# A windowed-attention and SwiGLU kernel: the opening's first loads, its attention with V stationary for six chunks, and its order rewritten

## The chip, the cores and the metric

The kernel runs on one NeuronCore of one Trainium2 chip. The metric is the device time of one execution in microseconds (us); lower is better. Engines are named as in the profile: PE (TensorE, matrix products), PEld (its weight loads), DVE (VectorE), ACT (ScalarE), POOL (GpSimd, which here makes the mask and issues the loads from HBM) and SP (SyncE, which issues the stores and the DMA transposes).

## The reference

Sliding-window causal attention over 8 sequences of 576 positions, 8 heads of 64, followed by a gated feed-forward block over the 4608 tokens. All inputs and the output are fp32.

```
scores = (q @ k^T) / 8, masked to 0 <= i - j < 64, softmax over j
x   = (softmax @ v), heads side by side: 4608 x 512
out = (silu(x @ w_gate) * (x @ w_val)) @ w_out        d_ff = 1536
```

## The kernel before

**Tiles.** The 4608 tokens are 36 chunks of 128 and nine token blocks of 512 (four chunks each). Matrix operands are bf16; the loads on POOL's queue convert on the way in.

**The steps of a chunk n**, each a method, with the lines that the profile shows:
- `load_qk`, `load_v` (L320, L382): three loads from HBM on POOL's queue. Chunks 0 and 1 differ: `first_loads` (L326) brings k and q of both as two fp32 transfers on SP's and ACT's queues, `first_cast` (L339, L337) converts them on DVE and ACT, `first_T` (L349) transposes them on PE.
- `T` (L407) transposes k and q on PE, with a copy out of PSUM on DVE or ACT (L339, L337); from chunk 8 on, `TD` (L420, L423) does it by two DMA transposes on SP's queue.
- `bias` (L431) writes the mask's large negative numbers into two PSUM banks ahead of the scores; it is used for chunks 0 to 3. Otherwise the mask is a multiplication on DVE after the exponential (L466).
- `S` (L451): 24 score matmuls on 64x64 quarters of the array into two banks; two exponentials on ACT (L461) give `pt`, keys on partitions.
- `A` (L500): 32 matmuls with `pt` stationary and V (with a column of ones) moving, so that queries lie on partitions and column 64 is the denominator. `A(n, n + 1)` puts the scores of the next chunk between its two halves. On DVE a reciprocal of four columns and a multiplication per half (L515, L518) give `xb`.
- `X` (L532) transposes `xb` on PE, with a copy to `xT` on ACT (L541); `XD` (L547) does it by a DMA transpose.

**The feed-forward part.** `F(c, f, t0, t1)` does one of twelve 128-wide slices of d_ff for tokens t0 to t1 of block c: four matmuls for gate and four for value (L565), then a tanh on ACT (L571) and two operations on DVE (L573, L575), which give `hT`. `O(c, u)` multiplies 128 tokens of `hT` by w_out in 12 matmuls (L589), copies on ACT (L601) and stores on SP's queue (L603). PSUM has eight banks; `banks` sets which are used in turn by attention ("a") and by F ("f").

**The order** is written out by hand in `build`, as a list of calls. Each engine runs its instructions in this order; a small planner in the kernel adds the semaphore waits that the tiles need. For blocks 0 and 1 the calls stand one by one; from block 2 on a loop places one chunk of attention, four chunks ahead, between F and O. `W(a, b)` loads gate and value slices a to b, `load_wo` loads w_out. Matmuls on zeros (`warm`, L368) run before the first data.

Of the kernel before, what the change touches and what calls it, by code (L numbers as in the profile page):

```python
# [5 lines left out]
ALU = mybir.AluOpType  # L6
# [188 lines left out]
class _Kernel:  # L195
# [8 lines left out]
    NO = 4  # L204

# [7 lines left out]
    def alloc(self):  # L213
# [20 lines left out]
        self.fq, self.fk = [sb(x, H * 128, F32)[:, :].rearrange("p (h j d) -> p h j d", h=H, j=2) for x in ("fq", "fk")]  # L234
        self.cq, self.ck = [sb(x, H * 128)[:, :].rearrange("p (j h d) -> p j h d", j=2, h=H) for x in ("cq", "ck")]
# [66 lines left out]
    def init_mask(self):  # L302
        for p0, c0, op in ((0, 0, ALU.is_ge), (0, 64, ALU.is_gt), (64, 0, ALU.is_gt), (64, 64, ALU.is_ge)):
            d = self.nmask[p0:p0 + 64, c0:c0 + 64]
            sg = 1 if op == ALU.is_gt else -1
            self.g.op("pool", lambda e, d=d, op=op, sg=sg: e.affine_select(
                out=d, in_=d, compare_op=op, fill=-30000.0, base=0,
                pattern=[[-sg, 64]], channel_multiplier=sg), writes=["nmask"])
        self.g.op("dve", lambda e: e.tensor_scalar(self.mask[:, :], self.nmask[:, :], -1.0, None, ALU.is_ge),
                  reads=["nmask"], writes=["mask"])  # L310
# [11 lines left out]
    def first_loads(self):  # L322
        for eng, dst, src, nm in (("sp", self.fk, self.k, "fk"), ("act", self.fq, self.q, "fq")):
            d = dst.rearrange("p h j d -> p h (j d)")
            a = src[0, :, 0:256, :].rearrange("h (p j) d -> p h (j d)", j=2)
            self.g.op(eng, lambda e, d=d, a=a: e.dma_start(d, a), writes=[nm], dma=True)  # L326

    def first_cast(self, which, half, eng):
        dst, src = (self.ck, self.fk) if which == "k" else (self.cq, self.fq)
        hs = slice(0, 8) if half is None else slice(4 * half, 4 * half + 4)  # L330
        d = dst[:, :, hs].rearrange("p j h d -> p h j d")
        wk = [("c" + which, i) for i in range(2) if half in (None, i)]
        self.move(eng, d, src[:, hs], ["f" + which], wk)
# [7 lines left out]
    def first_T(self, which):  # L341
        bank, bk = self.bank("a")
        tb = bank[:, :].bitcast(BF).rearrange("p (c j t) -> p c j t", c=4, j=2)
        src = self.ck if which == "k" else self.cq

        def pe(e):
            for pr in range(4):
                for j in range(2):
                    r = e.transpose(tb[:, pr, j, :], src[:, j, 2 * pr:2 * pr + 2, :], self.ident[:, :])  # L349
            return r  # L350

        self.g.op("pe", pe, reads=["ident", ("c" + which, 0), ("c" + which, 1)], writes=[bk])
# [42 lines left out]
    def T(self, n, keng="act"):  # L395
# [3 lines left out]
        parts = [("kn", self.kn[iq], kd, kk, keng), ("qn", self.qn[iq], self.qT[iz], qk, "act")]  # L399
        for group in ([parts] if keng == "act" else [parts[:1], parts[1:]]):  # L400
# [34 lines left out]
    def S(self, n, bb=None, defer=False):  # L435
# [33 lines left out]
        for f in masks:  # L469
            f()  # L470

# [78 lines left out]
    def F(self, c, f, t0=0, t1=512):  # L550
        g = self.g
        it, ih = c % self.NX, c % self.NH
        xT, hT = self.xT[it], self.hT[ih]
        i = self.n_s % self.NS
        self.n_s += 1
        sig, uu = self.sig[i], self.uu[i]
        n = t1 - t0
        xk = [("xT", it, u) for u in range(t0 // 128, t1 // 128)]
        G, gk = self.bank("f")
        V, vk = self.bank("f")  # L560
# [9 lines left out]
        g.op("pe", mm(G, self.Wg), reads=xk + [("Wg", f)], writes=[gk])  # L570
        g.op("act", lambda e: e.activation(sig[:, 0:n], G[:, 0:n], ACTF.Tanh, scale=0.5), reads=[gk], writes=[("sig", i)])  # L571
        g.op("pe", mm(V, self.Wv), reads=xk + [("Wv", f)], writes=[vk])
# [180 lines left out]
    def build(self):  # L753
# [7 lines left out]
        self.first_loads()  # L761
# [15 lines left out]
        self.load_v(4)
        load(5)
        W(10, 12)
        load(6)  # L780
        load(7)

        self.banks("a", [5, 6, 7, 4, 0, 1])
        self.warm(13)
        self.first_cast("k", None, "dve")
        self.first_cast("q", 0, "act")
        self.first_cast("q", 1, "dve")
        tk = self.first_T("k")
# [163 lines left out]
```

## Time and profile before

| | us |
|---|---|
| runs shown | 338.45, 336.24, 336.99 (median 336.99) |
| the profiled execution, its own time | 338.46 |
| its span, first to last instruction | 336.6 |
| first real matmul (transposes of chunk 0 and 1) | 6.94 |
| first F (0,0) | 14.01 |
| A(4,5) | 37.37 |
| F(2,0), first of the third token block | 86.99 |

How to read it: a timeline row gives start, duration, engine, line, operation, output and inputs, shape and count, and in brackets the idle time before it with what ended that. A row of the groups gives busy time in us and the mean in ns of one, then the idle time before. A row of windows gives for each engine the busy time and, after the five engines, the granted TensorE clock (1.00 is full), the busy share of the DMA engines and GB/s. A PE row's duration includes its drain, so back-to-back rows overlap.

### The profile page before, as it was taken

The numbers are of one execution on the slowest core, as the hardware profiler recorded it, in microseconds if no ns is written. First come the engines' busy times: TensorE is split into PE (matmuls) and PEld (weight loads), VectorE is DVE, ScalarE is ACT, GpSimd is POOL, SyncE is SP. The second block draws the span as 40 slices with busy tenths as digits, with TensorE's granted clock in tenths as the row PEclk, the third lists the DMA queues.
The fourth block names the chain that finished last, engine by engine and source line by source line (L and its number), as shares of the span: only waits on it lengthen the run. The fifth ranks groups of instructions, "written<-read, shape, count | busy, mean of one in ns | idle before, by whom it ended". The sixth has DMA issues, their size and how long they took to land.

```text
span 336.6 us, 8417 instructions
## 1 busy us (share of the span) xinstructions
PE 325.6 (97%) x3515; PEld 166.1 (49%) x3515; DVE 215.6 (64%) x481; ACT 140.1 (42%) x256; POOL 111.1 (33%) x141
## 2 busy tenths in 40 slices
PE   6979999998999999999999999999999999999995
PEld 3548567644444444444444444444444444444444
DVE  5548789478667766666666666666666665566510
ACT  2645874354444544443433344433443332332311
POOL 7999993463544353333343333000000000000000
PEclk9979999999999999999999999999999999999999
DMA  9999999999999999999999999334331111000012
GB/s 170 143 186 171 167 195 160 154 177 128 172 179 180 177 154 166 162 168 127 125 80 149 139 139 126 80 79 80 78 80 49 47 49 49 31 32 34 34 65 95
DMA packets 169516, 40.20 MB, mean 119 GB/s; under 512 B 155904, under 2 KB 164992, under 8 KB 169472
## 3 DMA queue, kind: packets, MB, share of 16 engines
q0 software_dynamic: 117312, 18.36, 77.6%
q1 hardware_dynamic: 50976, 20.66, 34.0%
q10 hardware_dynamic: 1184, 0.59, 0.7%
q8 instruction: 29, 0.48, 0.5%
q14 instruction: 15, 0.12, 0.2%
HBM read 37.75 MB, written 9.44 MB: 140 GB/s over the span
## 4 chain that ended last, share of the span: by engine, by line
PE 87%; DMA 4%; POOL 4%; DVE 2%; ACT 1%; issue 1%; SPq 0%; POOLq 0%
PE ps L565 53%; PE ps L589 26%; PE ps L500 4%; DMA qT<-qn 2%; PE ps L451 2%; DMA Wv<-in_moe_w_val_dram 2%; POOL va L382 1%; PE ps L617 1%; POOL Wg L388 1%; PE ps L407 1%; POOL Wv L388 1%; POOL qn L320 1%; POOL kn L320 1%; DVE uu L573 0%; PE ps L532 0%
## 5 line engine op out<-in xcount | busy, mean ns | idle before, releaser
L573 DVE SCALAR_TENSOR_TENSOR uu<-sig,ps 128x512 bf16<-128x512 bf16 (+2 forms) x122 | 76.1, 624 | 82.6 <-ACT sig L571 82.4
L565 PE MATMUL ps<-xT,Wg 128*128 128x512 bf16 (+2 forms) x488 | 114.1, 356 | 2.0 <-DMA Wg<-in_moe_w_gate_dram 0.9
L565 PE MATMUL ps<-xT,Wv 128*128 128x512 bf16 (+2 forms) x488 | 113.8, 356 | 0.7 <-DMA Wv<-in_moe_w_val_dram 0.7
L589 PE MATMUL ps<-Wo,hT 128*128 128x512 bf16 x420 | 95.9, 379 | 0.0
L571 ACT ACTIVATE sig<-ps 128x512 bf16<-128x512 f32 (+2 forms) x122 | 66.9, 549 | 61.6 <-PE ps L565 61.1
L575 DVE SCALAR_TENSOR_TENSOR hT<-uu,ps 128x512 bf16<-128x512 bf16 (+2 forms) x122 | 76.3, 625 | 5.2 <-PE ps L565 1.0
L565 PEld LDWEIGHTS ps<-xT,Wv 128*128 128x128 bf16 x488 | 47.3, 98 | 47.7 <-DMA Wv<-in_moe_w_val_dram 1.0
L589 PEld LDWEIGHTS ps<-Wo,hT 128*128 128x128 bf16 x420 | 41.0, 98 | 48.9
L565 PEld LDWEIGHTS ps<-xT,Wg 128*128 128x128 bf16 x488 | 43.9, 98 | 42.3 <-DMA Wg<-in_moe_w_gate_dram 1.0
L320 POOL DMA_DIRECT2D qn<-in_q_dram x38 | 35.1, 941 | 85.9 <-DMA qT<-qn 85.6
L601 ACT ACTIVATE ost<-ps 128x512 f32<-128x512 f32 x35 | 20.9, 597 | 95.1 <-PE ps L589 92.2
L461 ACT ACTIVATE pt<-ps 128x512 bf16<-128x512 f32 x72 | 38.9, 595 | 22.6 <-PE ps L451 22.6
L382 POOL DMA_DIRECT2D va<-in_v_dram x40 | 37.2, 940 | 1.0 <-issue 0.6
L320 POOL DMA_DIRECT2D kn<-in_k_dram x38 | 35.0, 927 | 5.0 <-DMA Wo<-in_moe_w_out_dram 4.0
L518 DVE TENSOR_TENSOR xb<-ps,rc 128x256 bf16<-128x256 f32 x72 | 30.6, 425 | 2.5
L466 DVE TENSOR_TENSOR pt<-pt,mask 128x512 bf16<-128x512 bf16 x64 | 24.1, 417 | 0.2 <-ACT pt L461 0.2
L500 PE MATMUL ps<-va,pt 64*64 64x65 bf16 x1088 | 23.3, 199 | 0.6
L500 PEld LDWEIGHTS ps<-va,pt 64*64 64x64 bf16 x1088 | 15.3, 109 | 16.1 <-issue 11.2
L515 DVE RECIPROCAL rc<-ps 128x4 f32<-128x4 f32 x72 | 12.6, 175 | 9.9 <-PE ps L500 9.9
L451 PE MATMUL ps<-qT,kT 64*64 64x64 bf16 (+1 forms) x864 | 15.9, 201 | 1.0 <-DMA qT<-qn 1.0
L451 PEld LDWEIGHTS ps<-qT,kT 64*64 64x64 bf16 x864 | 12.6, 108 | 3.1 <-DMA qT<-qn 1.2
L339 DVE COPY ost<-ps 128x128 f32<-128x128 f32 x1 | 0.3, 291 | 11.8 <-PE ps L617 11.8
(50 smaller groups left out, 72.5 us busy)
## 6 DMA issues: line engine op xcount, KB each, us to landing
out_dram<-ost SPq DMA_DIRECT2D x35, 256.0 KB, 3.1
va<-in_v_dram POOLq DMA_DIRECT2D x32, 128.0 KB, 9.9
qn<-in_q_dram POOLq DMA_DIRECT2D x30, 128.0 KB, 11.2
kn<-in_k_dram POOLq DMA_DIRECT2D x30, 128.0 KB, 10.0
Wo<-in_moe_w_out_dram POOLq DMA_DIRECT2D x2, 768.0 KB, 17.4
Wg<-in_moe_w_gate_dram POOLq DMA_DIRECT2D x5, 256.0 KB, 8.0
Wv<-in_moe_w_val_dram POOLq DMA_DIRECT2D x5, 256.0 KB, 9.1
fk<-in_k_dram SPq DMA_DIRECT2D x1, 512.0 KB, 5.4
```

What stands on the lines that cost most here:

```text
L320: self.g.op("pool", lambda e, d=d, a=a: e.dma_start(d, a), writes=ks, dma=True)
L382: g.op("pool", lambda e, d=d, a=a: e.dma_start(d, a), writes=ks, dma=True)
L451: r = e.matmul(sv[h][o:o + 64, c, q0:q1], self.kT[ps, c, kk:kk + 64], qT[ps, c, q0:q1], start=not biased, stop=not biased or c == 3 and kk ...
L461: g.op("act", lambda e, po=po, si=si: e.activation(po, si, ACTF.Exp, scale=SCALE), reads=[bk], writes=[pk])
L466: "dve", lambda e: e.tensor_tensor(po, po, m, ALU.mult), reads=[pk, "mask"], writes=[pk]))
L500: r = e.matmul(av[half][ws, j, :], pt[ks, h, ws], vv[ks, h, 0:65], start=key == q[0], stop=key == q[-1])
L518: g.op("dve", lambda e, xo=xo, rb=rb, a=av[half]: e.tensor_tensor(xo, a[:, :, 0:64], rb, ALU.mult), reads=[bk, ("rc", ir)], writes=[("xb", ...
L565: r = e.matmul(bank[:, 0:n], W[:, kk, f * 128:f * 128 + 128], xT[:, kk, t0:t1], start=(kk == 0), stop=(kk == NK - 1))
L571: g.op("act", lambda e: e.activation(sig[:, 0:n], G[:, 0:n], ACTF.Tanh, scale=0.5), reads=[gk], writes=[("sig", i)])
L573: g.op("dve", lambda e: e.scalar_tensor_tensor(uu[:, 0:n], sig[:, 0:n], 1.0, G[:, 0:n], ALU.add, ALU.mult), reads=[("sig", i), gk], writes ...
L575: g.op("dve", lambda e: e.scalar_tensor_tensor(hT[:, f, t0:t1], uu[:, 0:n], 0.5, V[:, 0:n], ALU.mult, ALU.mult), reads=[("uu", i), vk], wr ...
L589: r = e.matmul(OB[:, :], hT[:, f, 128 * u:128 * u + 128], self.Wo[:, f, :], start=(f == 0), stop=(f == NF - 1))
```

## The change

- **First loads.** Four transfers in place of two: k and q of chunk 0, then of chunk 1. One fp32 tile `fx` holds k on partitions 0 to 63 and q on 64 to 127 for one chunk. `open_T` transposes it by ordinary matmuls against half of the identity, into two fp32 banks; `open_ev` copies them to `kT` and `qT`.
- **The mask** is one select on POOL and two operations on DVE in place of four selects.
- **V stationary.** For chunks 0, 1, 2, 3, 6 and 7, `open_A` replaces `A` and `X`: V is the stationary operand and `pt` moves, so the result already lies as `xT` needs it. The denominators come from matmuls with ones, broadcast over 64 partitions: a 128x512 bank, whose reciprocal DVE takes whole (`dn`); two multiplications write `xT`. 32 matmuls of one column and a reciprocal of eight columns fill `rc`, which only a later check of the denominators reads.
- **Chunks 6 and 7** get their mask by `bias`, and their scores no longer stand inside another chunk's `A`. **Chunks 8 and 9** are transposed by PE (`T`) and no longer by `TD`.
- **F.** With at most 256 tokens, gate and value share one bank. With `defer`, the matmuls are issued where F stands and the work on ACT and DVE where `Fev` stands.
- **The order** of blocks 0 and 1, with the order of the loads, is written anew. Values and weights come in another order: two more weight transfers, chunk 8 behind w_out.

The diff, cut to its core; the removed calls of `build` are those printed above:

```diff
-        self.fq, self.fk = [sb(x, H * 128, F32)[:, :].rearrange("p (h j d) -> p h j d", h=H, j=2) for x in ("fq", "fk")]
-        self.cq, self.ck = [sb(x, H * 128)[:, :].rearrange("p (j h d) -> p j h d", j=2, h=H) for x in ("cq", "ck")]
+        self.fx = [t[:, :].rearrange("p (h j d) -> p h j d", h=H, j=2) for t in ring("fx", self.NG, H * 128, F32)]
+        self.cx = [t[:, :].rearrange("p (j h d) -> p j h d", j=2, h=H) for t in ring("cx", self.NG, H * 128)]
+        self.dn = ring("dn", 2, 512, F32)
...
+        g, nm = self.g, self.nmask
+        big = -2.0 ** 30
+        g.op("pool", lambda e: e.affine_select(
+            out=nm[:, :], in_=nm[:, :], compare_op=ALU.is_ge, fill=big, base=0,
+            pattern=[[1, 128]], channel_multiplier=-1), writes=["nmask"])
+        for p0 in (0, 64):
+            a = nm[p0:p0 + 64, p0:p0 + 64]
+            d = nm[p0:p0 + 64, 64 - p0:128 - p0]
+            g.op("dve", lambda e, d=d, a=a: e.tensor_scalar(d, a, -1.0, big, ALU.mult, ALU.add), reads=["nmask"], writes=["nmask"])
+        g.op("dve", lambda e: e.tensor_scalar(self.mask[:, :], nm[:, :], -1.0, None, ALU.is_ge),
+             reads=["nmask"], writes=["mask"])
...
+    def open_load(self, n, eng, which):
+        src, p0 = (self.k, 0) if which == "k" else (self.q, 64)
+        i = n % self.NG
+        d = self.fx[i][p0:p0 + 64].rearrange("p h j d -> p h (j d)")
+        a = src[0, :, 128 * n:128 * n + 128, :].rearrange("h (p j) d -> p h (j d)", j=2)
+        self.g.op(eng, lambda e: e.dma_start(d, a), writes=[("fx", i, which)], dma=True)
+
+    def open_cast(self, n, h0, h1, eng):
+        i = n % self.NG
+        d = self.cx[i][:, :, h0:h1].rearrange("p j h d -> p h j d")
+        self.move(eng, d, self.fx[i][:, h0:h1], [("fx", i, "k"), ("fx", i, "q")], [("cx", i, h) for h in range(h0, h1)])
...
+    def open_T(self, n):
+        i = n % self.NG
+        src = self.cx[i]
+        got = []
+        for w in range(2):
+            bank, bk = self.bank("a")
+            tb = bank[:, :].rearrange("p (c j t) -> p c j t", c=4, j=2)
+
+            def pe(e, tb=tb, w=w):
+                for pr in range(4):
+                    for j in range(2):
+                        r = e.matmul(tb[:, pr, j, :], src[:, j, 2 * pr:2 * pr + 2, :], self.ident[:, 64 * w:64 * w + 64],
+                                     start=True, stop=True)
+                return r
+
+            self.g.op("pe", pe, reads=["ident"] + [("cx", i, h) for h in range(H)], writes=[bk])
+            got.append((tb, bk))
+        return got
+
+    def open_ev(self, n, got, keng="dve", qeng="act"):
+        for (tb, bk), d, nm, eng in ((got[0], self.kT[:, :, 64 + 128 * n:192 + 128 * n], "kT", keng), (got[1], self.qT[n], "qT", qeng)):
+            a = tb.rearrange("p c j t -> p c t j")
+            self.move(eng, d.rearrange("p c (t j) -> p c t j", j=2), a, [bk], [(nm, n, p) for p in range(4)])
...
+    def open_A(self, n):
+        g = self.g
+        ip, it, u = n % self.NP, n // 4, n % 4
+        va, vp, pt = self.va[n % self.NV], self.va[(n - 1) % self.NV], self.pt[ip]
+        db, dk = self.bank("a")
+        bb = [self.bank("a") for _ in range(2)]
+        den = db[:, :].rearrange("p (c q) -> p c q", c=4)
+        out = [b[:, 0:256].rearrange("p (j q) -> p j q", j=2) for b, _ in bb]
+        tot = bb[0][0][:, 256:264]
+        po = pt.rearrange("p (c e) q -> p c e q", e=2)
+        lo = 0 if (2 * n) % BPB else 64
+        hi = 128 if (2 * n + 1) % BPB else 64
+        count, done = {}, {}
+
...
+        def den_seq(kp):
+            ks, qq = span(kp)
+            qq = qq if part else [slice(0, 128)]
+            return [(("d", e), den[64 * e:64 * e + 64, 2 * i:2 * i + 2, q], self.ones[ks, 0:64], po[ks, 2 * i:2 * i + 2, e, q])
+                    for i in range(2) for q in qq for e in range(2)]
+
+        def out_seq(step):
+            seq = []
+            for j in range(2):
+                for half in range(2):
+                    kp = half ^ step
+                    ks, qq = span(kp)
+                    c = 2 * half + j
+                    cuts = [(q, vp if kp and q.start == 0 else va) for q in qq]
+                    for e in range(2):
+                        for q, vv in cuts:
+                            seq.append(((half, e), out[half][64 * e:64 * e + 64, j, q], vv[ks, 2 * c + e, 0:64], po[ks, c, e, q]))
+            return seq
+
+        def tot_seq(kp):
+            ks = span(kp)[0]
+            return [((0, w), tot[64 * w:64 * w + 64, h:h + 1], pt[ks, h, 64 * w:64 * w + 64], self.ones[ks, 0:1])
+                    for h in range(H) for w in range(2) if kp == w or (2 * n + w) % BPB]
+
+        parts = [(den_seq(0), [dk]), (out_seq(0) + tot_seq(0), None), (den_seq(1), [dk]), (out_seq(1) + tot_seq(1), None)]
...
+        near = (n - 1, n) if n else (n,)
+        vk = [("va", m % self.NV, j) for m in near for j in range(2)] + [("va", m % self.NV) for m in near]
+        pk = [("pt", ip, 0), ("pt", ip, 1), "ones"]
+        ok = [bk for _, bk in bb]
+        prev = None
+        order = []
+        for i, (seq, wk) in enumerate(parts):
+            order.append(g.op("pe", run(seq), reads=pk + ([] if wk else vk), writes=wk or ok,
+                              after=[order[i - 2]] if i >= 2 else []))
+        dn = self.dn[n % 2]
+        g.op("dve", lambda e: e.reciprocal(dn[:, :], db[:, :]), reads=[dk], writes=[("dn", n % 2)])
+        dv = dn[:, :].rearrange("p (c q) -> p c q", c=4)
+        for half, (_, bk) in enumerate(bb):
+            cs = slice(2 * half, 2 * half + 2)
+            xo = self.xT[it][:, cs, 128 * u:128 * u + 128]
+            g.op("dve", lambda e, xo=xo, half=half, cs=cs: e.tensor_tensor(xo, out[half], dv[:, cs, :], ALU.mult),
+                 reads=[bk, ("dn", n % 2)], writes=[("xT", it, u)])
+        rc = self.rc[:, 8 * n:8 * n + 8]
+        g.op("dve", lambda e: e.reciprocal(rc, tot), reads=[ok[0]], writes=[("rc", 2 * n), ("rc", 2 * n + 1)])
...
+        if n <= 256:
+            G, gk = self.bank("f")
+            V = G[:, 256:512]
+            vk = gk
+        else:
+            G, gk = self.bank("f")
+            V, vk = self.bank("f")
...
+        g.op("pe", mm(V, self.Wv), reads=xk + [("Wv", f)], writes=[vk])
+        if defer:
+            return (c, f, t0, t1, i, G, gk, V, vk)
+        self.F_ev(c, f, t0, t1, i, G, gk, V, vk)
+
+    def F_ev(self, c, f, t0, t1, i, G, gk, V, vk):
...
-        self.first_loads()
+        self.open_load(0, "sp", "k")
+        self.open_load(0, "act", "q")
+        self.open_load(1, "sp", "k")
+        self.open_load(1, "sp", "q")
         self.init()
         self.init_pool_a()
         self.init_mask()
         self.load_v(0)
+        W(0, 1)
         self.load_v(1)
+        load(2)
         W(1, 2)
+        load(3)
+        W(2, 3)
+        W(3, 4)
+        W(4, 6)
+        load(4)
+        W(6, 8)
+        load(5)
         W(8, 10)
         W(10, 12)
         load(6)
         load(7)
         self.load_wo(0, 6)
         self.load_wo(6, 12)
+
+        def pre(n, *cast):
+            for h0, h1, eng in cast or ((0, 8, "dve"),):
+                self.open_cast(n, h0, h1, eng)
+
+        def att(n):
+            if n in self.FAST:
+                self.open_A(n)
+            else:
+                self.A(n)
+                self.X(n, "act")
+
+        def F(f, t0, t1, c=0):
+            held.append(self.F(c, f, 128 * t0, 128 * t1, True))
+
+        def Fev():
+            for h in held:
+                self.F_ev(*h)
+            held.clear()
+
+        held = []
+        bs = {}
+        self.banks("a", [5, 6, 7, 4, 0, 1])
+        self.banks("f", [2, 3])
+        self.warm(13)
+        pre(0, (0, 5, "dve"), (5, 8, "act"))
+        t = self.open_T(0)
+        bs[0] = self.bias(0)
+        self.open_ev(0, t)
+        self.S(0, bs[0])
+        self.warm(2)
+        pre(1)
+        t = self.open_T(1)
+        self.open_ev(1, t)
+        att(0)
+        bs[1] = self.bias(1)
+        self.S(1, bs[1])
+        F(0, 0, 1)
+        self.T(2, "dve", "act")
+        att(1)
+        Fev()
+        bs[2] = self.bias(2)
+        self.S(2, bs[2])
+        F(0, 1, 2)
+        F(1, 0, 2)
+        self.T(3, "dve", "act")
+        att(2)
+        Fev()
+        bs[3] = self.bias(3)
+        self.S(3, bs[3])
+        self.banks("f", [0, 1, 2, 3])
+        self.banks("a", [5, 6, 7, 4])
+        F(0, 2, 3)
+        F(1, 2, 3)
+        att(3)
+        Fev()
+        self.F(0, 2, 0, 384)
+        self.F(0, 3, 0, 384)
+        self.F(0, 0, 384, 512)
+        self.F(0, 1, 384, 512)
+        self.F(0, 2, 384, 512)
+        self.F(0, 3, 384, 512)
+        load(8)
         load(9)
+        self.F(0, 4)
         self.T(4)
         load(10)
+        self.F(0, 5)
+        self.S(4)
         self.F(0, 6)
+        self.F(0, 7)
         self.T(5)
         load(11)
+        self.F(0, 8)
         self.A(4, 5)
+        self.F(0, 9)
+        self.F(0, 10)
+        self.X(4, "act")
+        self.T(6, "dve", "act")
         load(12)
+        self.A(5)
+        self.F(0, 11)
+        self.T(7, "act", "dve")
         self.X(5, "act")
+        self.banks("a", [4, 5, 0, 1, 6, 7])
+        self.banks("f", [2, 3])
+        bs[6] = self.bias(6)
+        self.S(6, bs[6])
+        bs[7] = self.bias(7)
+        F(0, 0, 2, 1)
+        Fev()
+        self.S(7, bs[7])
+        F(1, 0, 2, 1)
+        att(6)
+        Fev()
+        F(2, 0, 2, 1)
+        att(7)
+        Fev()
+        self.banks("a", [4, 5, 0, 1])
+        self.banks("f", [3, 6, 7, 2])
+        F(3, 0, 2, 1)
+        for f in range(4):
+            F(f, 2, 4, 1)
+            Fev()
+        load(13)
+        self.T(8)
+        self.F(1, 4)
         self.S(8)
         self.TD(10)
         self.TD(11)
+        self.T(9)
+        self.F(1, 5)
+        self.O(0, 0, None, "f")
+        load(14)
+        self.A(8, 9)
+        self.XD(8)
+        self.TD(12)
+        self.F(1, 6)
+        self.O(0, 1, None, "f")
+        load(15)
+        self.A(9, 10)
+        self.XD(9)
+        self.TD(13)
+        self.F(1, 7)
+        self.F(1, 8)
+        load(16)
+        self.A(10, 11)
+        self.TD(14)
+        self.O(0, 2, None, "f")
+        self.X(10, "act")
+        self.F(1, 9)
+        load(17)
+        self.A(11, 12)
+        self.TD(15)
+        self.F(1, 10)
+        self.O(0, 3, None, "f")
+        self.X(11, "act")
+        self.F(1, 11)
...
```

177 lines of the change are left out of this document (38 added, 139 removed).

## The prediction

> **What bounds the kernel now.** I read the page's busy times and clock row first, then its chain of work that ended last, then a window that holds the opening's slow stretch and one that holds the rest.
>
> ```profile
> PE 325.6 (97%) x3515; PEld 166.1 (49%) x3515; DVE 215.6 (64%) x481; ACT 140.1 (42%) x256; POOL 111.1 (33%) x141
> ...
> PEclk9979999999999999999999999999999999999999
> ...
> PE 87%; DMA 4%; POOL 4%; DVE 2%; ACT 1%; issue 1%; SPq 0%; POOLq 0%
> ```
>
> ```profile
> 20.00:25.00 5.00, 4.13 (x80) 2.68 (x79) 2.59 (x10) 0.71 (x3) 5.00 (x8) 0.66 1.46 196
> 80.00:330.00 250.00, 249.92 (x2399) 118.09 (x2400) 159.36 (x325) 96.90 (x167) 50.34 (x60) 1.00 0.95 105
> ```
>
> From 80 us on TensorE is busy 249.92 of 250.00 us at full clock, and the change leaves that part as it is. Whatever happens must happen before the first pass of the third token block, F(2,0). So I compare when that pass starts, and carry the difference to the end. The first 80 us have these waits in the timeline of TensorE (bracketed), and these landmarks:
>
> ```profile
> 1.20 4.40 PE L368 MATMUL ps<-wz 128*128 128x512 bf16 x13 [1.20 <-DVE wz L282]
> ...
> 19.83 0.61 PE L565 MATMUL ps<-xT,Wg 128*128 128x256 bf16 x4 [0.91 <-DMA Wg<-in_moe_w_gate_dram]
> 21.16 1.04 PE L565 MATMUL ps<-xT,Wv 128*128 128x256 bf16 x4 [0.72 <-DMA Wv<-in_moe_w_val_dram]
> ...
> 37.37 0.25 PE L500 MATMUL ps<-va,pt 64*64 64x65 bf16 x6
> ...
> 38.01 1.04 PE L565 MATMUL ps<-xT,Wg 128*128 128x512 bf16 x4
> ...
> 50.11 0.40 PE L532 MATMUL ps<-ident,xb 128*128 128x128 bf16 x4 [0.25 <-DVE xb L518]
> 51.10 0.61 PE L565 MATMUL ps<-xT,Wg 128*128 128x256 bf16 x4 [0.60 <-DVE uu L573]
> ...
> 79.98 0.41 PE L451 MATMUL ps<-qT,kT 64*64 64x128 bf16 x22 [1.04 <-DMA qT<-qn]
> ...
> 86.99 1.03 PE L565 MATMUL ps<-xT,Wg 128*128 128x512 bf16 x4
> ```
>
> The 37.37 row is A(4,5), the 86.99 row F(2,0). The two DMA waits at 19 to 21 us go with the granted clock of 0.66 in that window. All that the change can remove from here is small: waits of 0.91, 0.72, 0.25, 0.60 and 1.04 us, and some clock.
>
> **The change part by part: the price that decides.** The new attention takes the reciprocal of a whole 128x512 fp32 bank on VectorE, six times (chunks 0 to 3, 6, 7). Before, a reciprocal had 4 columns. Call the new one R. The nearest rows of VectorE's groups:
>
> ```profile
> L573 DVE SCALAR_TENSOR_TENSOR uu<-sig,ps 128x512 bf16<-128x512 bf16 x96 | 65.8, 685 | 76.2 <-ACT sig L571 76.1
> L518 DVE TENSOR_TENSOR xb<-ps,rc 128x256 bf16<-128x256 f32 x72 | 30.6, 425 | 2.5
> L515 DVE RECIPROCAL rc<-ps 128x4 f32<-128x4 f32 x72 | 12.6, 175 | 9.9 <-PE ps L500 9.9
> L573 DVE SCALAR_TENSOR_TENSOR uu<-sig,ps 128x256 bf16<-128x256 bf16 x22 | 9.2, 419 | 5.7 <-ACT sig L571 5.6
> ...
> L573 DVE SCALAR_TENSOR_TENSOR uu<-sig,ps 128x128 bf16<-128x128 bf16 x4 | 1.1, 285 | 0.7 <-ACT sig L571 0.7
> ...
> L339 DVE COPY ost<-ps 128x128 f32<-128x128 f32 x1 | 0.3, 291 | 11.8 <-PE ps L617 11.8
> ...
> L642 DVE TENSOR_SCALAR flag<-low 1x1 int32<-1x1 f32 x1 | 0.1, 142 | 0.0
> ```
>
> The three L573 rows give (685 - 285) / 384 = 1.04 ns per column for a plain operation. The fixed part of an instruction is then 291 - 133 = 158 ns by the COPY from PSUM, and 142 ns by the one-column TENSOR_SCALAR. The four-column reciprocal, 175 ns, leaves 17 to 33 ns for four columns: 4.25 to 8.25 ns each, four to eight times the plain price. That gives R between 0.158 + 512 x 4.25 ns = 2.33 us and 0.142 + 512 x 8.25 ns = 4.37 us. The third reading is that the extra 13 ns over 158 + 4 x 1.04 belong to the instruction once: R = 0.171 + 512 x 1.04 ns = 0.70 us. I take the middle of the first two, 150 ns and 6.25 ns per column, R = 3.35 us, since the row is over the plain price under each fixed part that the trace offers; all three stay for the range.
>
> [...]
>
> **Prices on TensorE and ScalarE** (issue distance from one row to the next; a row's own length includes its drain):
>
> ```profile
> 14.01 0.40 PE L565 MATMUL ps<-xT,Wg 128*128 128x128 bf16 x4 [0.24 <-ACT xT L541]
> 14.24 0.39 PE L565 MATMUL ps<-xT,Wv 128*128 128x128 bf16 x4
> ...
> 17.04 0.59 PE L431 MATMUL ps<-nmask,ident 128*128 128x512 bf16 x2
> 17.56 0.44 PE L451 MATMUL ps<-qT,kT 64*64 64x128 bf16 x24
> ...
> 25.24 0.60 PE L565 MATMUL ps<-xT,Wg 128*128 128x256 bf16 x4
> 25.68 0.60 PE L565 MATMUL ps<-xT,Wv 128*128 128x256 bf16 x4
> ...
> 32.90 1.03 PE L565 MATMUL ps<-xT,Wg 128*128 128x512 bf16 x4
> 33.76 1.03 PE L565 MATMUL ps<-xT,Wv 128*128 128x512 bf16 x4
> ...
> 52.10 0.72 PE L500 MATMUL ps<-va,pt 64*64 64x65 bf16 x32
> 52.75 0.61 PE L565 MATMUL ps<-xT,Wg 128*128 128x256 bf16 x4
> ...
> 58.32 0.45 PE L451 MATMUL ps<-qT,kT 64*64 64x128 bf16 x24
> 58.70 2.76 PE L589 MATMUL ps<-Wo,hT 128*128 128x512 bf16 x12
> ```
>
> ```profile
> 25.93 0.38 ACT L571 ACTIVATE sig<-ps 128x256 bf16<-128x256 f32 x1
> ```
>
> ```profile
> L461 ACT ACTIVATE pt<-ps 128x512 bf16<-128x512 f32 x72 | 38.9, 595 | 22.6 <-PE ps L451 22.6
> ```
>
> So an F (gate and value) costs 0.46, 0.88 and 1.72 us at 128, 256 and 512 tokens, by interpolation 1.3 at 384; a T, eight transposes of the same 128 columns, 0.46, and an X, four, 0.23; a bias pair 0.52; S 0.38; A 0.65. A(4,5) with S(5) inside is 38.01 - 37.37 = 0.64, so an interleaved S is free. From the last issue of a PE group to its reader, 25.93 - 25.68 = 0.25 us.
>
> The new attention, open_A, has 64 matmuls for an inner chunk: 8 of 256 columns for the denominators, 24 of 64 or 128 for the output, 32 of one column. It is at least the old A, 0.65. Counted in columns (512 columns cost 0.216 us by the 32.90 rows): the denominators go two side by side, 8 x 0.108 / 2 = 0.43; the outputs four side by side, 0.22; the single columns 32 x 0.64 / 56 = 0.37, by the spacing of the 56 matmuls in A(4,5). That sums to 1.02 us; I take 0.85.
>
> **First chunk.** The first two loads are made four; chunk 0's k (SP) and q (ScalarE's queue) are half as many bytes as before, chunk 1's follow on SP and are cast while S(0) runs:
>
> ```profile
> fk<-in_k_dram SPq DMA_DIRECT2D x1, 512.0 KB, 5.4
> ...
> fq<-in_q_dram ACTq DMA_DIRECT2D x1, 512.0 KB, 6.3
> ```
>
> Issued at 0.76 us they land between half of that time (3.5) and unchanged (7.1); I take 5.3. Cast 0.5; the warm-up matmuls end at 5.6 anyway. Sixteen transposes of 64 columns, 0.46 to 0.92, take 0.6: till 6.4. Drain 0.25 and the copies (0.69, 0.6): 7.3. S 0.38, drain, two exponentials of 0.6: 9.1. open_A(0) 0.85 and drain: the first reciprocal starts at 10.2. Behind it stand two multiplications of 0.425 on the same queue. So xT(0) is ready at 11.05 + R.
>
> **The loop over chunks 0 to 3.** TensorE is in order, and the held F of chunk n (it waits for xT(n)) stands in front of T(n+2) and open_A(n+1). So one hand-over is F + T + open_A + 0.25 + R + 0.85:
> - xT(0) to xT(1): 0.46 + 0.46 + 0.85 + 0.25 + R + 0.85 = 2.87 + R
> - to xT(2): F of 128 and 256 tokens, 1.34 instead of 0.46: 3.75 + R
> - to xT(3): two F of 128, no T: 0.92 + 0.85 + 0.25 + R + 0.85 = 2.87 + R
>
> xT(3) is ready at 20.54 + 4R. F(0,3) then waits for banks 0 and 1, whose evacuation stands behind the reciprocal on VectorE (0.2 + 2 x 0.285 = 0.77); then 1.3, four F of 128 (1.84), five of 512 (8.6), two T, S(4): 13.81. A(4,5) starts at 34.35 + 4R, against 37.37 before. That is even at R = 0.76.
>
> **From A(4,5) to F(2,0)**: 86.99 - 37.37 = 49.62 before. Taken off: 0.25 + 0.60 + 1.04 = 1.89, the DMA wait for qT(12) because attention now runs later behind the same loads. Added on TensorE: four bias banks 1.04; S(6) and S(7) no longer inside an A, 0.76; two open_A for two A and X, 2 x (0.85 - 0.65 - 0.23) = -0.06; chunks 8 and 9 transposed here, 0.92. Then a new stall: reciprocal 7 stands behind reciprocal 6, its multiplications, 0.2, and an evacuation of 0.84; xT(7) comes 2.99 + 2R after open_A(6), TensorE has 0.88 + 0.85 + 0.88 = 2.61 of work. Stall 0.38 + 2R. Sum: 49.62 + 0.77 + 0.38 + 2R.
>
> F(2,0) starts at 34.35 + 4R + 50.77 + 2R = 85.12 + 6R, against 86.99: **a difference of 6R - 1.87 us**. At R = 3.35 that is +18.2.
>
> **Clock.** TensorE then idles R + 1.1 - 0.9 (bias and S run meanwhile) = 3.55 us in each hand-over; before, 0.91 and 0.72 us were followed by a window of 0.66. TensorE's share of the loop is 0.85 + 1.77 + 2.65 + 1.77 = 7.0 us; at 0.66 it takes half as long again, +3.5; ends 0 (clock stays) and +7 (half clock).
>
> [...]
>
> **What I cost at nothing.** The gate and value loads ahead of F(0,3) carry the same bytes as those ahead of the row at 21.16, and F(0,3) starts at 20.54 + 2.8 + 0.77 = 24.1 us even at R = 0.70; if that cover failed, a wait for Wv would stand in front of F(0,3). POOL issues two more weight DMAs, one mask select instead of four; VectorE makes the rest of the mask while it waits for the first load. On POOL, loads of chunk 8 go behind Wo:
>
> ```profile
> 35.69 1.97 POOL L393 DMA_DIRECT2D Wo<-in_moe_w_out_dram  x2
> ```
>
> ```profile
> Wo<-in_moe_w_out_dram POOLq DMA_DIRECT2D x2, 768.0 KB, 17.4
> ```
>
> Wo's second half lands near 36.5 + 17.4 = 54 before; swapped, the loads of chunk 8 land there. T(8) comes after A(4,5), three F of 512 and eight of 256, two T, two X, A(5), two bias pairs, two S, two open_A and the stall: 37.2 + 20.2 = 57 us at R = 0.70, later with a larger R. Without that cover the wait would be Wo's, up to some 3 us. SP loses four DMA transposes (TD(8), TD(9)); XD and TD behind them only come sooner. ScalarE loses six copies of X.
>
> **Sum.** 18.2 + 3.5 = +21.7 us. The profiled execution took 338.46 us (span 336.6), the median of three runs is 336.99; I put the difference on the median: 358.7, say 358.
>
> **Rivals.**
> 1. *One column per cycle, not slower.* The extra of the 4-column row is paid once, R = 0.70: 6 x 0.70 - 1.87 = +2.3, 339.3 us; with open_A at the old A's 0.65 it is near 338. The clock term is gone, since idling is 0.9 us per hand-over. For it: the fixed part is known only to 16 ns, and 13 ns decide. Against it: every fixed part in the trace is below 175 - 4. It decides below R = 0.87 (+1%); the sign turns at 0.31. Faster by over 1% would need some 6 us more than this sum, from the earlier start and the waits that it has already counted.
> 2. *Eight times the plain price.* R = 4.37: +24.4, with the clock 3.5 to 7: 365 to 368 us. For it the one-column row; against it the COPY. [...]
> 3. *The weights, not VectorE, set the opening* as at 21.16: then the difference would be within +-1.6 us of none whatever R is. Against it: the loop above ends 10 us after those bytes have landed. Counted with rival 1.
>
> **Chances.** Main case (R of 2.3 to 4, 349 to 363 us) 0.43; rival 2 0.20; rivals 1 and 3 together 0.37, of which 0.12 faster by over 1% (prices that no row shows), 0.24 within, 0.01 slower. About 1% is what a measurement of this kernel can tell from no change. Faster 0.12, within 1% 0.24, slower 0.64. The slow case's own range is 349 to 367. The range over both signs is 336 to 365: below lies most of the faster case, above the upper part of rival 2.
>
> **What would show it.** Right: six RECIPROCAL rows of 128x512 near 3.35 us; TensorE idle in front of the held F by about 3.5 us, released by VectorE's xT; A(4,5) near 48 us; a clock of 0.5 to 0.8 between 12 and 36 us. Wrong: a reciprocal under 1 us, with A(4,5) near 37.

## The result, and the profile after

The changed kernel takes 361.78 us (median of 4 runs, 359.83 to 362.41), the kernel before on the same chip 336.95 us (4 runs): a ratio of 1.072, 95% interval 1.066 to 1.078. That is 24.8 us slower; the prediction was 358, with a range of 336 to 365. The profiled execution after took 362.34 us, its span is 360.5.

The page's busy times, its clock row and the shares of its chain of work by engine:

```profile
PE 340.2 (94%) x3696; PEld 173.0 (48%) x3696; DVE 233.6 (65%) x475; ACT 137.5 (38%) x249; POOL 111.6 (31%) x140
...
PEclk9956599969999999999999999999999999999999
...
PE 89%; DVE 7%; DMA 2%; SPq 0%; issue 0%; ACT 0%
```

TensorE's modelled busy time rose by 14.6 us, to be read with the clock row: the third to fifth slices and the ninth (18 to 45 us, 72 to 81 us) were granted 0.5 or 0.6. DVE's part of the chain went from 2% to 7%, and POOL's 4% is gone. The reciprocals are in VectorE's groups:

```profile
L443 DVE RECIPROCAL dn<-ps 128x512 f32<-128x512 f32 x6 | 20.1, 3356 | 5.7 <-PE ps L428 5.7
L606 DVE RECIPROCAL rc<-ps 128x4 f32<-128x4 f32 x60 | 10.5, 175 | 5.3 <-PE ps L591 5.3
L451 DVE RECIPROCAL rc<-ps 128x8 f32<-128x8 f32 x6 | 1.2, 198 | 0.0
```

Six of 3356 ns; TensorE ends the idle time before them. The timeline of TensorE at the landmarks:

```profile
15.80 0.40 PE L660 MATMUL ps<-xT,Wg 128*128 128x128 bf16 x4 [2.85 <-DVE xT L448]
...
22.57 0.61 PE L660 MATMUL ps<-xT,Wg 128*128 128x128 bf16 x4 [2.12 <-DVE xT L448]
...
31.63 0.61 PE L660 MATMUL ps<-xT,Wg 128*128 128x128 bf16 x4 [2.88 <-DVE xT L448]
...
39.80 1.46 PE L660 MATMUL ps<-xT,Wg 128*128 128x384 bf16 x4 [1.57 <-DVE hT L680]
...
44.93 1.03 PE L660 MATMUL ps<-xT,Wg 128*128 128x512 bf16 x4
...
55.03 0.25 PE L591 MATMUL ps<-va,pt 64*64 64x65 bf16 x6
...
67.12 0.30 PE L428 MATMUL ps<-pt,ones 64*64 64x256 bf16 x2
...
68.41 0.61 PE L660 MATMUL ps<-xT,Wg 128*128 128x256 bf16 x4
...
73.12 0.61 PE L660 MATMUL ps<-xT,Wg 128*128 128x256 bf16 x4 [2.39 <-DVE hT L680]
...
77.18 1.04 PE L660 MATMUL ps<-xT,Wg 128*128 128x256 bf16 x4 [3.01 <-DVE xT L448]
...
111.80 1.03 PE L660 MATMUL ps<-xT,Wg 128*128 128x512 bf16 x4
```

Each held F (15.80, 22.57, 31.63) waits for the `xT` that the reciprocal delays, and so do the two F passes of block 1 behind open_A(6) and open_A(7). The 39.80 row, F(0,3), and the 73.12 row wait through an evacuation queued behind the reciprocal. The 67.12 and 68.41 rows enclose open_A(6): 1.29 us, granted 1.00. Its reciprocal starts before its last matmuls are issued:

```profile
68.06 3.36 DVE L443 RECIPROCAL dn<-ps 128x512 f32<-128x512 f32 x1 [0.89 <-PE ps L428]
```

F(2,0) starts at 111.80 instead of 86.99, 24.8 us later; behind it TensorE is busy as before (238.12 of the 238.20 us up to 350, against 242.93 of the 243.01 us up to 330), and the rest of the span is 0.9 us shorter (360.5 - 111.80 against 336.6 - 86.99), which no run explains.

### The profile page after: what moved, and what is told of

Same layout as the page of the kernel before. It is cut to its first block, busy times and chain, and to the rows that moved or that the text cites. A ratio compares the mean times of both kernels' runs of the same rounds, so it can differ in the third digit from the quotient of the medians.

```text
span 360.5 us, 8743 instructions
## 1 busy us (share of the span) xinstructions
PE 340.2 (94%) x3696; PEld 173.0 (48%) x3696; DVE 233.6 (65%) x475; ACT 137.5 (38%) x249; POOL 111.6 (31%) x140
## 4 chain that ended last, share of the span: by engine, by line
PE 89%; DVE 7%; DMA 2%; SPq 0%; issue 0%; ACT 0%
PE ps L660 54%; PE ps L694 25%; DVE dn L443 6%; PE ps L591 3%; PE ps L541 2%; DMA fx<-in_q_dram 2%; PE ps L428 2%; DVE xT L448 1%; PE ps L497 1%; PE ps L722 1%; SPq L333 0%; PE ps L521 0%; PE ps L623 0%; DVE cx L344 0%; PE ps L357 0%
## 5 line engine op out<-in xcount | busy, mean ns | idle before, releaser
L660 PE MATMUL ps<-xT,Wg 128*128 128x512 bf16 (+3 forms) x476 | 117.4, 372 | 14.8 <-DVE xT L448 10.9
L678 DVE SCALAR_TENSOR_TENSOR uu<-sig,ps 128x512 bf16<-128x512 bf16 (+3 forms) x119 | 75.5, 634 | 84.7 <-ACT sig L677 84.4
L660 PE MATMUL ps<-xT,Wv 128*128 128x512 bf16 (+3 forms) x476 | 116.8, 370 | 0.0
L677 ACT ACTIVATE sig<-ps 128x512 bf16<-128x512 f32 (+3 forms) x119 | 66.3, 558 | 79.8 <-PE ps L660 79.3
L680 DVE SCALAR_TENSOR_TENSOR hT<-uu,ps 128x512 bf16<-128x512 bf16 (+3 forms) x119 | 75.9, 637 | 4.4 <-PE ps L660 0.3
L660 PEld LDWEIGHTS ps<-xT,Wv 128*128 128x128 bf16 x476 | 47.8, 103 | 49.6 <-issue 1.2
L609 DVE TENSOR_TENSOR xb<-ps,rc 128x256 bf16<-128x256 f32 x60 | 25.5, 425 | 2.1
L443 DVE RECIPROCAL dn<-ps 128x512 f32<-128x512 f32 x6 | 20.1, 3356 | 5.7 <-PE ps L428 5.7
L591 PE MATMUL ps<-va,pt 64*64 64x65 bf16 x904 | 19.1, 197 | 0.4 <-ACT xT L632 0.2
L591 PEld LDWEIGHTS ps<-va,pt 64*64 64x64 bf16 x904 | 12.4, 106 | 13.1 <-issue 11.9
L606 DVE RECIPROCAL rc<-ps 128x4 f32<-128x4 f32 x60 | 10.5, 175 | 5.3 <-PE ps L591 5.3
```

Source lines behind the costliest of these rows:

```text
L443: g.op("dve", lambda e: e.reciprocal(dn[:, :], db[:, :]), reads=[dk], writes=[("dn", n % 2)])
L591: r = e.matmul(av[half][ws, j, :], pt[ks, h, ws], vv[ks, h, 0:65], start=key == q[0], stop=key == q[-1])
L609: g.op("dve", lambda e, xo=xo, rb=rb, a=av[half]: e.tensor_tensor(xo, a[:, :, 0:64], rb, ALU.mult), reads=[bk, ("rc", ir)], writes=[("xb", ...
L660: r = e.matmul(bank[:, 0:n], W[:, kk, f * 128:f * 128 + 128], xT[:, kk, t0:t1], start=(kk == 0), stop=(kk == NK - 1))
L678: g.op("dve", lambda e: e.scalar_tensor_tensor(uu[:, 0:n], sig[:, 0:n], 1.0, G[:, 0:n], ALU.add, ALU.mult), reads=[("sig", i), gk], writes ...
L680: g.op("dve", lambda e: e.scalar_tensor_tensor(hT[:, f, t0:t1], uu[:, 0:n], 0.5, V[:, 0:n], ALU.mult, ALU.mult), reads=[("uu", i), vk], wr ...
```

## The experiments

All times are medians beside runs of the kernel before on the same chip (337.27 us for the first four; 337.34 for the spread reciprocal and the two groups of chunks; 337.81 for the run with 7 warm-up matmuls and for the part put into the kernel before). The changed kernel itself had 336.95 us beside it, so a difference from it is uncertain by some tenths of a us. Two theories of the prediction stood against two others: (A) the length of the whole-bank reciprocal on the hand-over from chunk to chunk, and (B) the clock that drops in these waits; against (C) the rest of the change, its order, loads and matmuls, and (D) a clock that is low where TensorE is not on the path anyway.

**A copy instead of the reciprocal.** The division is left out.

```diff
-        g.op("dve", lambda e: e.reciprocal(dn[:, :], db[:, :]), reads=[dk], writes=[("dn", n % 2)])
+        g.op("dve", lambda e: e.tensor_copy(dn[:, :], db[:, :]), reads=[dk], writes=[("dn", n % 2)])
```

> The changed kernel with a plain copy of the 128x512 bank in place of each of the six whole-bank reciprocals; the division of the attention is left out, everything else stays. If the length of the reciprocal on the hand-over from one chunk to the next is the cause: one such instruction falls from 3.36 to about 0.69 us, six of them give 16.0 us back, and TensorE, idle for under 1 us in front of each held F, keeps its clock and gives back up to 7 us more (F of 128 columns at 0.22 us a half again instead of 0.42): 339 to 346 us. If the rest of the change costs it (the order, the loads, the matmuls of open_A): 355 us or more. If the clock does not recover although the waits are short: 345 to 347 us.

342.13 us, ratio 1.013 (1.009 to 1.016): 19.7 us less than the changed kernel, by one instruction's length. Six shorter instructions alone are 16.0 us, so A holds; the rest falls to B, which the fillers below test by itself. C is left with 4.9 us over the kernel before. The timeline of TensorE shows what is left:

```profile
13.13 0.40 PE L660 MATMUL ps<-xT,Wg 128*128 128x128 bf16 x4 [0.19 <-DVE xT L448]
...
17.16 0.24 PE L428 MATMUL ps<-pt,va 64*64 64x128 bf16 x2 [1.91 <-issue]
...
18.50 0.61 PE L660 MATMUL ps<-xT,Wg 128*128 128x128 bf16 x4
...
91.56 1.03 PE L660 MATMUL ps<-xT,Wg 128*128 128x512 bf16 x4
```

The held F waits 0.19 us and no longer 2.85. A pause of 1.91 us remains inside open_A(1), with a slower F behind it (18.50: 0.61 us long, where the 13.13 row has 0.40; from 15 to 20 us the clock is 0.85, from 20 to 25 us 0.81). F(2,0) is at 91.56, 4.6 us behind the kernel before. TensorE's work up to that pass, in the windows of the kernel before and then of this run:

```profile
0.00:86.99 86.99, 79.43 (x1154) 48.99 (x1155) 59.08 (x164) 45.92 (x93) 64.57 (x86) 0.98 1.79 166
```

```profile
0.00:91.56 91.56, 83.56 (x1324) 50.49 (x1336) 60.78 (x158) 43.23 (x86) 68.07 (x88) 0.98 1.89 170
```

4.1 us more work at the same mean clock, and 0.4 us more idling. The parts of that work by rows: open_A 1.29 against A and X 0.88, six times, 2.5; bias 1.04, scores 0.76 and two T 0.92 as predicted; three warm-up matmuls fewer, -0.65: 4.6 us. So C is mostly more matmuls; the pauses here and the kernel before's own waits weigh about the same. This split is argued from the rows; no run took these parts out one by one.

**The reciprocal twice**, the first time into a tile that nobody reads:

```diff
+        g.op("dve", lambda e: e.reciprocal(self.dn[2][:, :], db[:, :]), reads=[dk], writes=[("dn", 2)])
```

> The changed kernel with each whole-bank reciprocal done twice, the first time into a tile that nobody reads. If the reciprocal lies on the hand-over chain all six times, with nothing beside it: 6 x 3.36 = 20.1 us more, 382 us (380 to 386, the clock being halved already in these stretches). If something else ends the waits (banks, loads, the exponentials), a part of the second instruction is hidden: under 372 us.

381.65 us, ratio 1.130 (1.126 to 1.135): 19.9 us more than the changed kernel, against 6 x 3.36 = 20.1. The sum is that of six instructions with nothing beside them. Its six waits:

```profile
19.29 0.61 PE L661 MATMUL ps<-xT,Wg 128*128 128x128 bf16 x4 [5.45 <-DVE xT L449]
...
30.09 0.61 PE L661 MATMUL ps<-xT,Wg 128*128 128x128 bf16 x4 [5.33 <-DVE xT L449]
...
41.59 0.61 PE L661 MATMUL ps<-xT,Wg 128*128 128x128 bf16 x4 [6.09 <-DVE xT L449]
...
52.97 1.46 PE L661 MATMUL ps<-xT,Wg 128*128 128x384 bf16 x4 [4.78 <-DVE hT L681]
...
89.25 1.04 PE L661 MATMUL ps<-xT,Wg 128*128 128x256 bf16 x4 [5.60 <-DVE hT L681]
...
96.51 1.03 PE L661 MATMUL ps<-xT,Wg 128*128 128x256 bf16 x4 [5.38 <-DVE xT L449]
```

The first of these rows comes 3.5 us later than in the changed kernel, and from one to the next the run takes between 2.4 and 4.0 us more (10.80 against 6.77 us in the first hand-over, 11.50 against 9.06 in the second). So the second instruction shows in each of the six places; the single places also hold shifts of the clock (from 15 to 20 us 0.50 here, 0.67 in the changed kernel), and only the sum is near 20.1.

**No chunk on open_A**, all else as changed:

```diff
-    FAST = (0, 1, 2, 3, 6, 7)
+    FAST = ()
```

> The changed kernel with no chunk on open_A: all six by A and X, at the same places of the new order, with the new loads, mask, bias and F. If open_A's reciprocal is the cause: the chain of one chunk is A 0.65, drain 0.25, two reciprocals of four columns and two multiplications 1.2, X 0.23, drain 0.25, copy 0.6 = 3.2 us where open_A takes 0.95 + 0.25 + 3.36 + 0.8 = 5.4 us; six times 2.2 = 13 us less, and 3 to 7 us of clock: 341 to 349 us. If the rest of the change costs it: 355 us or more.

344.80 us, ratio 1.020 (1.016 to 1.024). Also on the side of A; but it is not back at the time before, because in this order X follows A at once. The first and last of its six waits for `xb`:

```profile
12.72 0.61 PE L623 MATMUL ps<-ident,xb 128*128 128x128 bf16 x4 [1.29 <-DVE xb L609]
...
60.75 0.40 PE L623 MATMUL ps<-ident,xb 128*128 128x128 bf16 x4 [1.45 <-DVE xb L609]
```

Six such waits are 7.9 us. The old order had put T, F or warm-up matmuls between A and X.

**The waits filled** with matmuls on zeros, 12 behind S(1), S(2) and S(3), 10 and 13 in chunks 6 and 7:

```diff
         self.S(1, bs[1])
+        self.warm(12, "a")
...
         att(7)
+        self.warm(10, "a")
         Fev()
...
         F(3, 0, 2, 1)
+        self.warm(13, "a")
```

> The changed kernel with matmuls on zeros (128x512, 0.216 us each at full clock) on TensorE where it waits for the reciprocal: 12 behind S(1), S(2) and S(3), 10 and 13 behind open_A(7) and the F behind it. The waits themselves stay. If the halved clock behind each wait costs by itself: what TensorE does at half clock on the path (22.6 to 27.4 us, 31.6 to 35.0, 39.8 to 44.0, 77.2 to 81.4) comes back, some 6 to 7 us: 355 us (353 to 358). If the clock is a bystander because the path goes through VectorE in these stretches: 361 to 364 us, the fillers adding at most 0.5 us per wait.

355.25 us, ratio 1.052 (1.047 to 1.057): more work on TensorE, and 6.5 us faster than the changed kernel. B holds, D falls. The windows after the change, and with the fillers:

```profile
15.00:20.00 5.00, 4.20 (x92) 3.04 (x96) 2.91 (x5) 0.77 (x2) 5.00 (x8) 0.67 2.04 168
20.00:25.00 5.00, 2.88 (x40) 2.32 (x35) 3.04 (x6) 1.08 (x2) 5.00 (x8) 0.50 1.89 175
25.00:30.00 5.00, 3.75 (x100) 2.75 (x98) 3.00 (x2) 2.13 (x5) 5.00 (x8) 0.80 1.91 176
30.00:35.00 5.00, 3.37 (x66) 2.99 (x68) 2.85 (x8) 0.55 (x2) 5.00 (x7) 0.54 1.55 193
35.00:40.00 5.00, 3.43 (x37) 1.64 (x28) 4.89 (x8) 0.49 (x1) 5.00 (x6) 0.50 2.25 162
40.00:45.00 5.00, 5.00 (x41) 3.73 (x40) 3.38 (x9) 1.32 (x4) 0.13 (x1) 0.60 1.48 198
```

```profile
20.00:25.00 5.00, 4.82 (x87) 3.17 (x86) 2.94 (x8) 1.13 (x4) 5.00 (x8) 1.00 1.88 176
...
35.00:40.00 5.00, 4.19 (x31) 3.34 (x32) 3.94 (x13) 1.05 (x3) 5.00 (x6) 0.66 2.22 161
```

Only 35 to 40 us is still low, 0.66: the wait in front of F(0,3) had no filler there. The held passes of this run, and F(2,0):

```profile
15.81 0.40 PE L660 MATMUL ps<-xT,Wg 128*128 128x128 bf16 x4 [0.16 <-DVE xT L448]
...
21.94 0.40 PE L660 MATMUL ps<-xT,Wg 128*128 128x128 bf16 x4 [0.18 <-DVE xT L448]
...
29.09 0.40 PE L660 MATMUL ps<-xT,Wg 128*128 128x128 bf16 x4 [0.18 <-DVE xT L448]
...
35.81 0.82 PE L660 MATMUL ps<-xT,Wg 128*128 128x384 bf16 x4 [2.97 <-DVE hT L680]
...
50.66 0.25 PE L591 MATMUL ps<-va,pt 64*64 64x65 bf16 x6
...
105.42 1.03 PE L660 MATMUL ps<-xT,Wg 128*128 128x512 bf16 x4
```

At full clock (1.00 in the windows from 15 to 30 us) the first two hand-overs last 6.13 and 7.15 us. F(0,3) comes 4.0 us earlier than at 39.80, A(4,5) (the 50.66 row) 4.4 us earlier than at 55.03, and F(2,0) 6.4 us earlier than at 111.80.

**Another way to divide.** The single-column denominators first; a reciprocal of 8 columns; eight matmuls that spread it over the partitions into the freed bank; ScalarE copies the products meanwhile.

```diff
-        parts = [(den_seq(0), [dk]), (out_seq(0) + tot_seq(0), None), (den_seq(1), [dk]), (out_seq(1) + tot_seq(1), None)]
+        parts = [(tot_seq(0), [dk]), (tot_seq(1), [dk]), (out_seq(0), None), (out_seq(1), None)]
...
+                    x = e.matmul(den[64 * j:64 * j + 64, c, :], rb[:, h:h + 1].to_broadcast([128, 64]), self.ident[:, :],
+                                 start=c == 0, stop=c == 3)
```

> The changed kernel with another way to divide: the 32 single-column matmuls (denominators, queries on partitions) come first, their reciprocal has 8 columns (0.20 us), a copy to bf16 follows, and 8 matmuls (that reciprocal stationary, one column repeated over 64, the identity moving) spread it over the partitions into the bank that held the denominators; ScalarE copies the attention products to SBUF meanwhile, and VectorE multiplies the two. The denominator matmuls of 256 columns and the whole-bank reciprocals are gone; nothing of the result is left out. If the length of the reciprocal is the cause, the hand-over now ends on TensorE itself: matmuls 0.35 + 0.5 + 0.3, then bias and scores 0.9 while VectorE and ScalarE finish at 2.5 us from the start of open_A, so a wait of some 0.3 us and no drop of the clock: 336 to 342 us, 339 as the middle, at or under the run with the plain copy. If something else in the new order holds it back: 350 us or more.

344.22 us, ratio 1.017 (1.011 to 1.023). The long reciprocal is replaced without leaving anything out and 17.6 us come back, but the time lies 2 us over the range expected. No held F waits any more; yet the granted clock falls:

```profile
10.00:15.00 5.00, 4.15 (x106) 3.12 (x107) 2.45 (x6) 1.91 (x5) 5.00 (x7) 0.84 2.24 162
15.00:20.00 5.00, 4.87 (x101) 3.37 (x98) 2.07 (x7) 1.85 (x5) 5.00 (x8) 0.50 2.07 170
20.00:25.00 5.00, 4.86 (x90) 3.83 (x80) 0.87 (x3) 1.68 (x3) 5.00 (x7) 0.64 1.86 177
```

From 15 to 20 us TensorE is busy 4.87 of 5.00 us and is granted 0.50.

**The same with 7 warm-up matmuls** instead of 2 behind S(0):

```diff
-        self.warm(2)
+        self.warm(7)
```

> The run with the spread reciprocal of 8 columns, with 7 instead of 2 warm-up matmuls behind S(0), where TensorE waits for the load of chunk 1 (1.05 us idle). In that run TensorE has no wait over 0.4 us from 11 to 30 us and still is at half clock from 13.3 to 23.3 us, which costs it 3.6 us of work. If the pause and the short matmuls before 13.3 us are what lets the clock drop: it stays up and 340 to 342 us results. If the many matmuls of one column and 64 rows alone lower it: 344 us as before. The 5 added matmuls last 1.1 us at full clock, which the wait covers but for 0.1 us.

343.26 us, ratio 1.016 (1.012 to 1.019); its interval overlaps that of the run without. The clock stays full until 15 us, and then a pause that no wait explains stands inside the matmuls of open_A(1), before the clock falls to 0.86 and 0.79; windows, then timeline:

```profile
10.00:15.00 5.00, 4.70 (x123) 3.31 (x123) 2.36 (x7) 2.58 (x7) 5.00 (x7) 1.00 2.26 165
15.00:20.00 5.00, 3.84 (x100) 2.81 (x101) 1.65 (x7) 2.32 (x6) 5.00 (x8) 0.86 2.05 167
20.00:25.00 5.00, 4.32 (x82) 3.07 (x80) 1.62 (x4) 1.72 (x6) 5.00 (x8) 0.79 1.87 176
```

```profile
17.28 0.31 PE L429 MATMUL ps<-pt,va 64*64 64x64 bf16 x10 [1.02 <-issue]
```

Whether the early pause sets the clock is left inconclusive by this.

**The two groups of chunks apart:** FAST = (0, 1, 2, 3), and FAST = (6, 7).

> The changed kernel with open_A for chunks 0 to 3 only; 6 and 7 by A and X at the same places. In the changed kernel these two cost waits of 2.39 and 3.01 us, 1.7 us of half clock behind the second, and 2 x 1.29 us of matmuls; A and X would cost 2 x 0.88 us and waits of 1.30 and 1.45 us (as in the run without open_A): 5.2 us less, 356.6 us (355 to 358). If the waits of chunks 6 and 7 were covered by other work: 360 to 363 us.

> The changed kernel with open_A for chunks 6 and 7 only, chunks 0 to 3 by A and X. By the same sum, 5.2 us above the run with no open_A at all (344.8): 350 us (348.5 to 351.5). If the two groups of chunks are independent, this run and the one with chunks 0 to 3 add up to the changed kernel plus the run without open_A: 361.8 + 344.8 = 706.6 us. If what costs it is confined to the first loop: 345 to 346 us.

355.73 us (1.052, 1.047 to 1.058) and 351.68 us (1.039, 1.032 to 1.046); the second is 0.2 us over the range expected. Against the run with none (344.80), open_A costs 10.9 us in chunks 0 to 3 and 6.9 in 6 and 7; the two runs add up to 707.4, the sum expected was 706.6. The difference of 0.8 us is within the spread of these runs: neither group hides the other's cost.

**One small part of the change in the kernel before:** slices 2 and 3 of the weights as two transfers each.

```diff
-        for f in range(2, 8, 2):
+        W(2, 3)
+        W(3, 4)
+        for f in range(4, 8, 2):
             W(f, f + 2)
```

> The kernel before, with one piece of the change alone: the gate and value weights of d_ff slices 2 and 3 come as two transfers of 128 KB each instead of one of 256 KB. In the kernel before, F(0,2) waits 0.91 us for its gate slice and 0.72 us for its value slice, and the granted clock is 0.66 in that window. If these waits are worth what they last: the first transfer lands 0.8 us (128 KB at 165 GB/s) earlier and the second 1.5 us, so both waits go: 1.0 to 1.6 us, and up to 1 us of clock: 334.5 to 336.3 us. If the bytes ahead of them, not the size of the piece, set the landing, or the next wait takes their place: no difference, 336.8 to 337.8 us.

337.43 us, ratio 0.999 (0.997 to 1.001): no difference that these runs can tell; the interval leaves room for a gain of about 1 us. The two waits are gone and the granted clock from 20 to 25 us is 1.00 instead of 0.66, but other waits stand right behind them:

```profile
22.21 0.40 PE L532 MATMUL ps<-ident,xb 128*128 128x128 bf16 x4 [0.36 <-DVE xb L518]
...
24.09 0.61 PE L565 MATMUL ps<-xT,Wv 128*128 128x256 bf16 x4 [0.74 <-DMA Wv<-in_moe_w_val_dram]
```

No variant of the changed kernel came under the time before; the nearest that computes everything is 1.6% above it.

## Why the prediction was right, point by point

The mechanism and its price were right. F(2,0) was forecast 21.7 us later and came 24.8 us later. The 3.1 us between are the first chunk and the clock, less a stretch behind A(4,5) that was priced too long; the rest of the distance from 358 to 361.8 is the rounding of 358.7 to 358. The range of 336 to 365 held both signs, so the time alone says little: what was put to the test is the main case, with its chance of 0.43.

- **The price of the reciprocal: right.** R = 3.35 was taken from between 2.33 and 4.37; it is 3.356. That it lies far above the plain price was argued from the rows; that it hits the middle of the two readings is luck, since the rows left all between them open. The rows of 4, 8 and 512 columns give 5.75 and 6.26 ns per column and some 150 ns once. So rival 2 (4.37 us) falls, and rival 1 (0.70 us) too.
- **Each reciprocal on the path, six times: right.** The doubling adds 19.9 us, and some in each place.
- **The first chunk: 1.4 us too early.** xT(0) was put at 14.4; F starts at 15.80. The transposes began at 7.03 and not at 5.8, and open_A(0) stood behind the transposes of chunk 1, which waited 0.84 us for their cast, and the cast for its load of q; the prediction said that this cast runs beside S(0), and left out that open_A(0) queues behind what needs it.
- **The hand-overs: right at full clock.** 2.87 + R = 6.2 and 3.75 + R = 7.1 were forecast; with the fillers they are 6.13 and 7.15, without them 6.77 and 9.06 (the timeline's F at 15.80, 22.57, 31.63).
- **The wait in front of the held F:** 3.55 us forecast, 2.12 to 2.88 measured, since open_A's last matmuls run beside the reciprocal, and in front of the 22.57 row also because the bias and the scores that run meanwhile took longer at the lower clock: 0.96 us from the bias to the scores, where the stretch in front of the 15.80 row has 0.54 (18.86 to 20.46 us was granted 0.50).
- **A(4,5):** 47.8 us and 3.5 for the clock, 51.3; measured 55.03. Of the 3.7 missing, 1.4 are the first chunk; most of the rest is the clock behind the loop: between the 39.80 and the 44.93 rows stand F of 384 columns and four of 128, 3.14 us by the prices, in 5.13 us, granted 0.59.
- **A(4,5) to F(2,0):** 50.77 + 2R = 57.5 forecast, 111.80 - 55.03 = 56.8 measured, which is luck, a cancellation: with the fillers it is 105.42 - 50.66 = 54.8. The waits are 2.39 + 3.01 = 5.4 us and not 0.38 + 2R = 7.1, while a clock of 0.50 behind the second (77.18 to 81.40 us), which was not forecast there, adds 2.0.
- **The clock: the term that was mis-sized.** 3.5 us was taken, for the loop alone, with ends of 0 and 7. There it was nearly right: with the fillers F(0,3) starts at 35.81 and not at 39.80, so the loop lost 4.0 us. The factor 0.66, taken from the kernel before, was an average that happened to fit (there 21.16 to 24.50 us was granted 0.50); from 15 to 35 us the windows were granted between 0.50 and 0.80. What went wrong is how far the term reaches. The lower clock behind the loop was put at nothing and cost twice 2.0 us: the 5.13 us for 3.14 above, and the stretch from A(4,5) to F(2,0). That makes some 8 us in all. The fillers give 6.5 of it back; the rest, in the one window that they leave low, is read from the rows and shown by no run. The upper end of 7, half a clock for all of the loop, stands against these 4.0 us. The waits in front of the held F and of the 77.18 row were 2.12 to 3.01 us long. That idling of 0.9 us costs no clock, as rival 1 has it, is shown by no run: with no chunk on open_A, and waits of 1.29 and 1.30 us, the windows from 10 to 20 us were granted 0.73 and 0.93, those from 20 to 45 us 1.00.
- **open_A: under-priced, and it mattered little.** 0.85 was taken, below its own sum of 1.02; granted 1.00, it is 1.29 us (67.12 to 68.41). While the reciprocal is long, it starts before open_A's last matmuls: 0.94 us behind open_A's start (67.12 to 68.06), where 0.85 + 0.25 was forecast. With the copy, the whole 1.29 us counts. That run is 4.9 us over the time before, where the formula 6R - 1.87 gives 2.3 at R = 0.69; the longer open_A, the later first chunk (F at 13.13) and the pause of 1.91 us are more than enough for the difference, and no run divides them.
- **What was costed at nothing** stayed so: up to F(2,0) the profile names no wait of TensorE for a weight, a load of POOL's queue or a transfer of SP's behind the first chunk. Rival 3, the weights as the bound, is out: with the loads unchanged, the copy alone takes 19.7 us off.

## What to carry to other kernels

Before a reduction's result is spread over partitions ahead of a division, price the division by its columns: the reciprocal here cost some 6.26 ns for each column of the tile, although 64 partitions held the same value, and moving the broadcast behind the division made 8 columns of 512. An order written around one form of a step does not suit another: with the old attention in the new order, six waits of 1.3 us appeared. And a wait on TensorE can have a second price: here there were six, 14.8 us in all, and filling five of them with matmuls on zeros gave 6.5 us back.

## What the runs showed of the hardware

- The reciprocals of fp32 from PSUM took 175 ns for 4 columns, 198 for 8 and 3356 for 512: some 6.26 ns per column, against 1.04 for the plain operation of the L573 rows.
- The clock was also low without a wait: with the spread reciprocal it was 0.50 from 15 to 20 us, where TensorE was busy 4.87 of 5.00 us, after a stretch of short matmuls of one column and a pause of 1.05 us. What lowered it stays open.
- TensorE paused for 1.91 us (with the copy) and 1.02 us (with the warm-up matmuls) in the middle of a group of matmuls, with no wait that the profile shows. The rows of the two timelines add up to 220 and 222 matmuls in front of the pause, nearly the same count in two different programs; with the spread reciprocal and 2 warm-up matmuls no such pause stands there. What it waited for stays open.
